# Retention scores as 64x64 matmuls in the four quarters of the TensorE array

## The chip, the core and the metric

The kernel runs on one core of one Trainium2 chip. The metric is the device time of one execution in microseconds; lower is better. Times are the median of several executions. A profiled execution is one more execution, with its own time and a trace of every instruction.

## What is computed

Three stages follow each other: a retention (attention with a decayed state) over 4 batches, 8 heads, 768 steps and 64 dimensions a head, and two feed-forward blocks over the 3072 tokens. Only the retention is touched by the change.

```python
gamma = 1.0 - 2.0 ** (-5.0 - np.arange(H, dtype=np.float32))
scale = 1.0 / np.sqrt(D)
for t in range(S):
    state = gamma[None, :, None, None] * state + np.einsum('bhd,bhe->bhde', k[:, :, t], v[:, :, t])
    y[:, :, t] = scale * np.einsum('bhd,bhde->bhe', q[:, :, t], state)
...
x = np.ascontiguousarray(attn_out.transpose(0, 2, 1, 3)).reshape(B * S, H * D)
x = _moe_ref(x=x, **moe_kwargs)
return _moe2_ref(x=x, **moe2_kwargs)
```

## The kernel before

The retention is done in 24 units: 4 batches of 6 chunks of 128 steps, all 8 heads of a chunk together. A unit's inputs are one tile `unit` of 1 MB: q and k transposed (the first half, one load of 512 KB), then k and v by tokens (the second half, another). SyncE's queue issues the loads (L478). Five such tiles exist (`UNITS`), and the load of unit u+4 is issued when unit u-1 has been used up, so four units' loads can be outstanding. The same 16 DMA engines also carry the weights of the first feed-forward block (`raw`, L123, from GpSimd's queue).

What TensorE does, in program order, is `scores(0)`, `scores(1)`, `outputs(0)`, `scores(2)`, `outputs(1)` and so on:

- `scores(u)` (L487): eight f32 matmuls, one for each head, k transposed (64 rows by 128 columns) against q transposed (64 by 128). Heads lie in pairs, one in rows 0 to 63 of the array (a = 0, results in one PSUM bank), the other in rows 64 to 127 (a = 1, the other bank). The result tile `sc` has one buffer. VectorE multiplies it by the causal mask into `pt` (L496), which also frees `sc`.
- `outputs(u)`: eight matmuls of `vs` with `pt` (L544, 128 rows by 64 columns), eight that add to the state `dp` (L555, 128 by 64; left out in the last chunk of a batch), and eight of the state `st` with q (L566, 64 by 64; left out in the first chunk of a batch). In L566 two successive heads pairs use all four quarters of the array: (rows 0-63, columns 0-63), (64-127, 64-127), (64-127, 0-63), (0-63, 64-127).

Each f32 matmul shows in the trace as two weight loads and two matmuls, so eight of them make 16 records of each. `vs` (v with its decay factors) is made by ScalarE in eight pieces of one head (L511), or by GpSimd (L506) in some units. `st` is a copy of `dp` by ScalarE (L560). VectorE scales the output `yp` (L579, L583, L586) and, from unit 12 on, spends most of the rest on converting the weights (L134, L139, L147, L167).

After the last unit the first feed-forward block starts on TensorE with L643, and from there on TensorE works through matmuls of 128x128 by 512 columns to the end.

Of the kernel before, what the change touches and what calls it, by code (L numbers as in the profile page):

```python
# [60 lines left out]
def tile_retention_then_two_ffns(  # L61
# [10 lines left out]
    nc = tc.nc  # L72
# [368 lines left out]
    with tc.manual_schedule():  # L441

        with (
# [36 lines left out]
            def scores(u):  # L480
                t = units[u]
                qk = t[:, 0:1024].rearrange("p (b n a i) -> p b n a i", b=2, n=2, a=2)
                v = t[:, 1536:2048].rearrange("p (h e) -> p h e", h=H)
                sc = aps.tile([P, 2, NP, P], F32, tag="sc", name=f"sc{u}", bufs=1)
                for p in range(NP):
                    for a in range(2):
                        nc.tensor.matmul(  # L487
                            sc[:, a, p, :],
                            qk[64 * a:64 * a + 64, p // 2, 1, p % 2, :],
                            qk[64 * a:64 * a + 64, p // 2, 0, p % 2, :],  # L490
                            start=True, stop=True,
                        )
                pt = att.tile([P, 2, NP, P], F32, tag="pt", name=f"pt{u}")

                def masked():
                    nc.vector.tensor_tensor(  # L496
                        out=pt.rearrange("p r a i -> p (r a) i"),
                        in0=sc.rearrange("p r a i -> p (r a) i"),
                        in1=mask_sb.unsqueeze(1).to_broadcast([P, H, P]),
                        op=ALU.mult,  # L500
                    )

                vs = att.tile([P, H, D], F32, tag="vs", name=f"vs{u}")
                if u < CPB or u % 3 == 0:

                    nc.gpsimd.tensor_tensor(  # L506
                        out=vs, in0=v, in1=vtab_sb[:, u % CPB, :].unsqueeze(2).to_broadcast([P, H, D]), op=ALU.mult
                    )
                else:
                    for h in range(H):  # L510
                        nc.scalar.mul(vs[:, h, :], v[:, h, :], vtab_sb[:, u % CPB, h:h + 1])  # L511
                pend[u] = (pt, vs)
                return masked
# [87 lines left out]
            for u in range(NU + 1):  # L601
                cv_high()
                masked = scores(u) if u < NU else None
                if u == 0:
                    fill = aps.tile([P, 2, NP, P], F32, tag="yp", name="fill")
                    for i in range(FILL):
                        nc.tensor.matmul(fill[:, 0, :, :], warm_sb[:, 0:P], warm_sb, start=True, stop=True)
                low = split_0()
                scaled = outputs(u - 1) if u > 0 else None
                if 0 < u < CPB:  # L610
                    for p in range(NP):
                        nc.scalar.mul(ytab_sb[u][:, p, :], ytab_sb[0][:, p, :], ystep_sb[:, u, p:p + 1])
                if masked is not None:
                    masked()
                if low is not None:
                    low()
                cv_unit(u)
                if scaled is not None:
                    scaled()
                cv_ahead(u)  # L620
                if u > 0:
                    load_unit(u + UNITS - 1)
# [141 lines left out]
        for n in range(NSTD):  # L764
            for f in range(NF):
# [8 lines left out]
                if n == 0 and f in (2, 3):  # L774
                    j = XHELD + f - 2
# [381 lines left out]
```

## Time and profile before

| what | value |
|---|---|
| three runs | 1040.97, 1044.02, 1045.16 us; median 1044.02 |
| the profiled execution | 1041.52 us, span of its trace 1039.8 us |
| granted TensorE clock | 1.0 of full speed throughout |
| busy, share of the span | TensorE matmul 99%, VectorE 73%, ScalarE 54%, GpSimd 12% |
| retention | from about 5 us to 82.7 us of the span |

An engine's busy time here is the union of its instructions' times. A busy TensorE is not one at its peak: a matmul's record runs from its start to the end of its pipeline, and the next may start long before that. How fast matmuls follow each other is therefore read from the starts: a merged row of 16 records that lasts 1.16 us, one record being 0.27 us, has 0.89 us from the first start to the last.

### The profile page before, as it was taken

Reading aid. Unit: us, or ns where it says so; the run is one execution under the profiler, and the core shown is the slowest. Engines: PE = TensorE matmul, PEld = TensorE weight load, DVE = VectorE, ACT = ScalarE, POOL = GpSimd, SP = SyncE. Lnnn points to the kernel's source line nnn. Section 1 sums busy time; section 2 is a strip of 40 time slices with the busy share of each in tenths; the row PEclk is TensorE's granted clock in tenths of the full one; section 3 lists DMA queues with packets and bytes.
Section 4 is the critical chain, followed back from the end, with each engine's and each line's share of the span. In section 5 each row is a group of like instructions: output and inputs, shape, how many; then the busy total and the mean of one; then the engine's idle time right before and its main releaser. Section 6 shows DMA issues by size and latency. Waiting matters only on the chain.

```text
span 1039.8 us, 15581 instructions
## 1 busy us (share of the span) xinstructions
PE 1028.8 (99%) x5602; PEld 849.1 (82%) x5602; DVE 762.5 (73%) x1059; ACT 559.1 (54%) x906; POOL 119.7 (12%) x183
## 2 busy tenths in 40 slices
PE   9999999999999999999999999999999999999998
PEld 6888888888888888888788888788888888888886
DVE  5798998798898888567787566887445986355953
ACT  4677775344766365556455688464233464234442
POOL 3121210111333000112000111000100001000000
PEclk9999999999999999999999999999999999999999
DMA  9995898865898867999867898767866667776664
GB/s 348 404 404 174 270 313 298 308 229 223 268 349 286 312 208 227 329 338 351 276 213 229 309 369 299 272 210 236 296 193 194 203 204 229 219 194 193 207 198 162
DMA packets 114637, 274.04 MB, mean 264 GB/s; under 512 B 12160, under 2 KB 12288, under 8 KB 114304
## 3 DMA queue, kind: packets, MB, share of 16 engines
q1 hardware_dynamic: 87008, 171.32, 50.0%
q0 software_dynamic: 26976, 100.67, 27.6%
q8 instruction: 45, 0.74, 0.3%
q10 hardware_dynamic: 576, 1.05, 0.3%
q14 instruction: 32, 0.26, 0.1%
HBM read 199.59 MB, written 73.40 MB: 263 GB/s over the span
## 4 chain that ended last, share of the span: by engine, by line
PE 82%; DMA 2%; DVE 0%; issue 0%
PE D L843 36%; PE X L843 16%; PE Z L843 8%; PE Y L843 4%; PE h L797 3%; PE h L795 3%; PE h L796 3%; DMA r<-kw 2%; PE y L676 2%; PE y L674 2%; PE y L675 2%; PE h L643 2%; PE h L645 1%; PE h L644 1%; DVE o L981 0%
## 5 line engine op out<-in xcount | busy, mean ns | idle before, releaser
L843 PE MATMUL D<-gx,r 128*128 128x512 f32 x1680 | 383.7, 390 | 2.9 <-DMA r<-kw 2.9
L843 PEld LDWEIGHTS D<-gx,r 128*128 128x128 f32 x1680 | 314.7, 188 | 70.8 <-DMA r<-kw 4.6
L947 DVE TENSOR_TENSOR gx<-g,gx 128x1024 fp32r<-128x1024 f32 x140 | 170.6, 1221 | 49.8 <-ACT gx L946 49.2
L946 ACT CAST gx<-g 128x1024 fp32r<-128x1024 f32 x140 | 145.1, 1050 | 110.2 <-PE D L843 97.4
L843 PE MATMUL X<-xh,r 128*128 128x512 f32 x512 | 157.7, 389 | 0.0
L864 ACT COPY g<-X 128x512 f32<-128x512 f32 x96 | 56.3, 586 | 154.6 <-PE X L843 154.4
L869 DVE TENSOR_TENSOR g<-Z,g 128x512 f32<-128x512 f32 x64 | 44.2, 691 | 123.0 <-ACT g L864 93.6
L843 PEld LDWEIGHTS X<-xh,r 128*128 128x128 f32 x512 | 96.0, 188 | 20.1 <-ACT g L864 0.2
L843 PE MATMUL X<-xl,r 128*128 128x512 f32 x256 | 99.6, 389 | 0.0
L843 PE MATMUL Z<-xh,r 128*128 128x512 f32 x256 | 78.8, 389 | 0.0
L843 PEld LDWEIGHTS Z<-xh,r 128*128 128x128 f32 x256 | 48.0, 188 | 10.0
L843 PEld LDWEIGHTS X<-xl,r 128*128 128x128 f32 x256 | 48.1, 188 | 10.0
L643 PE MATMUL h<-hl,w 128*128 128x512 f32 x128 | 50.2, 392 | 0.4 <-DVE w L167 0.4
L644 PE MATMUL h<-hl,w 128*128 128x512 f32 x128 | 49.9, 390 | 0.0
L645 PE MATMUL h<-hl,w 128*128 128x512 f32 x128 | 49.8, 389 | 0.0
L676 PE MATMUL y<-gl,w 128*128 128x512 f32 x128 | 49.8, 389 | 0.0
L674 PE MATMUL y<-gh,w 128*128 128x512 f32 x128 | 49.8, 389 | 0.0
L675 PE MATMUL y<-gh,w 128*128 128x512 f32 x128 | 49.8, 389 | 0.0
L795 PE MATMUL h<-hl,w 128*128 128x512 f32 x128 | 49.8, 389 | 0.0
L796 PE MATMUL h<-hl,w 128*128 128x512 f32 x128 | 49.8, 389 | 0.0
L797 PE MATMUL h<-hl,w 128*128 128x512 f32 x128 | 49.8, 389 | 0.0
L843 PE MATMUL Z<-xl,r 128*128 128x512 f32 x128 | 49.8, 389 | 0.0
(107 smaller groups left out, 1604.5 us busy)
## 6 DMA issues: line engine op xcount, KB each, us to landing
r<-kw SPq DMA_DIRECT2D x504, 256.0 KB, 3.0
kw<-wq POOLq DMA_DIRECT2D x32, 896.0 KB, 6.5
unit<-qkv SPq DMA_DIRECT2D x48, 512.0 KB, 9.0
raw<-w POOLq DMA_DIRECT2D x32, 512.0 KB, 6.3
kw<-wh POOLq DMA_DIRECT2D x16, 1024.0 KB, 4.7
kw<-w SPq DMA_DIRECT2D x16, 512.0 KB, 5.0
raw<-win POOLq DMA_DIRECT2D x16, 512.0 KB, 6.5
raw<-wout POOLq DMA_DIRECT2D x16, 512.0 KB, 7.2
```

The costliest lines, as they stand in the source:

```text
L643: nc.tensor.matmul(hp, lo[:, k], xh, start=(k == 0), stop=False)
L644: nc.tensor.matmul(hp, hi[:, k], xh, start=False, stop=False)
L645: nc.tensor.matmul(hp, hi[:, k], xl, start=False, stop=(k == KD - 1))
L674: nc.tensor.matmul(a, lo[:, e], gh, start=s0, stop=False)
L675: nc.tensor.matmul(a, hi[:, e], gh, start=False, stop=False)
L676: nc.tensor.matmul(a, hi[:, e], gl, start=False, stop=s1)
L795: nc.tensor.matmul(hp, lo[:, k], xh, start=(k == 0), stop=False)
L796: nc.tensor.matmul(hp, hi[:, k], xh, start=False, stop=False)
L797: nc.tensor.matmul(hp, hi[:, k], xl, start=False, stop=(k == KD - 1))
L843: nc.tensor.matmul(a, w, b, start=start, stop=stop, skip_group_check=True)
L946: nc.scalar.copy(out=hi, in_=src)
L947: v.tensor_tensor(out=lo, in0=src, in1=hi, op=ALU.subtract)
```

## The change

Each of the eight score matmuls of a unit (64 rows, 128 columns) becomes two of 64 rows by 64 columns. The first half gives output partitions 0 to 63, the second 64 to 127, from the same q. The order is: head pair, then row half a, then column half j. A unit's scores thus take 16 matmuls (32 records) in place of eight (16 records), and each pair of heads uses all four quarters of the array. What the matmuls write and where is the same, and no other line is changed; the changed file is one line longer.

```diff
                 for p in range(NP):
                     for a in range(2):
-                        nc.tensor.matmul(
-                            sc[:, a, p, :],
-                            qk[64 * a:64 * a + 64, p // 2, 1, p % 2, :],
-                            qk[64 * a:64 * a + 64, p // 2, 0, p % 2, :],
-                            start=True, stop=True,
-                        )
+                        for j in range(2):
+                            nc.tensor.matmul(
+                                sc[64 * j:64 * j + 64, a, p, :],
+                                qk[64 * a:64 * a + 64, p // 2, 1, p % 2, 64 * j:64 * j + 64],
+                                qk[64 * a:64 * a + 64, p // 2, 0, p % 2, :],
+                                start=True, stop=True, skip_group_check=True,
+                            )
```

On TensorE's queue a middle unit of the retention reads so before (a row is a line, the tile written and those read, the output's partitions by columns, how many in a row, and what is waited for):

```order
L566 MATMUL yp_307<-unit_160,st_267 64x128 x8
L487 MATMUL sc_348<-unit_167 128x128 [waits DMAHW2_49,DVE_49]
L487 MATMUL sc_348<-unit_167 128x128 x7
L544 MATMUL yp_364<-pt_300,vs_301 64x128 [waits Pool_49]
L544 MATMUL yp_364<-pt_300,vs_301 64x128 x7
```

and in the changed kernel:

```order
L567 MATMUL yp_339<-unit_160,st_291 64x128 x8
L488 MATMUL sc_380<-unit_167 64x128 [waits DMAHW2_49,DVE_49]
L488 MATMUL sc_380<-unit_167 64x128 x15
L545 MATMUL yp_404<-pt_332,vs_333 64x128 [waits Pool_49]
L545 MATMUL yp_404<-pt_332,vs_333 64x128 x7
```

Nothing moved: the scores stand between the same neighbours, and their first matmul still waits for a load of the unit (DMAHW) and for VectorE, which frees `sc`.

## Rows read from the trace of the kernel before

**Rows 1.** The page's busy time, share of the span and instructions of each engine.

```profile
PE 1028.8 (99%) x5602; PEld 849.1 (82%) x5602; DVE 762.5 (73%) x1059; ACT 559.1 (54%) x906; POOL 119.7 (12%) x183
```

**Rows 2.** Stretches of 4 us: each engine's busy time, clock, DMA share, GB/s.

```profile
28.00:32.00 4.00, 4.00 (x76) 3.69 (x74) 3.06 (x6) 3.08 (x13) 0.00 (x0) 1.00 1.02 403
...
68.00:72.00 4.00, 3.45 (x72) 3.05 (x72) 3.96 (x7) 4.00 (x14) 0.00 (x0) 1.00 1.03 407
76.00:80.00 4.00, 4.00 (x85) 3.64 (x82) 3.62 (x5) 3.83 (x16) 0.41 (x1) 1.00 1.00 390
80.00:84.00 4.00, 4.00 (x72) 3.20 (x69) 3.53 (x7) 2.67 (x7) 0.53 (x1) 1.00 0.32 111
```

**Rows 3.** TensorE's matmul groups, 0 to 83 us: busy us, mean ns | idle before.

```profile
L487 PE MATMUL sc<-unit 64*128 64x128 f32 x384 | 28.5, 286 | 2.1 <-DMA unit<-qkv 1.4 <-DVE w L167 0.5
L544 PE MATMUL yp<-pt,vs 128*64 128x128 f32 x384 | 26.3, 279 | 0.0
...
L566 PE MATMUL yp<-unit,st 64*64 64x128 f32 x320 | 13.3, 282 | 0.0
```

**Rows 4.** Timeline, units 21 to 23: start, length, engine, instructions [idle before].

```profile
71.51 1.16 PE L487 MATMUL sc<-unit 64*128 64x128 f32 x16 [0.55 <-DMA unit<-qkv]
...
74.09 0.67 PE L566 MATMUL yp<-unit,st 64*64 64x128 f32 x16
...
74.69 0.97 PEld L487 LDWEIGHTS sc<-unit 64*128 64x128 f32 x16 [0.17 <-DVE hm L139]
74.69 1.16 PE L487 MATMUL sc<-unit 64*128 64x128 f32 x16
...
75.78 1.09 PE L544 MATMUL yp<-pt,vs 128*64 128x128 f32 x16
...
75.90 1.23 DVE L496 TENSOR_TENSOR pt<-sc,tab_sb 128x1024 f32<-128x1024 f32 x1
...
76.71 0.64 PE L555 MATMUL dp<-vs,unit 128*64 128x64 f32 x16
...
77.27 0.67 PE L566 MATMUL yp<-unit,st 64*64 64x128 f32 x16
...
77.87 1.16 PE L487 MATMUL sc<-unit 64*128 64x128 f32 x16
...
78.63 2.02 ACT L511 ACTIVATE vs<-unit,tab_sb 128x64 f32<-128x64 f32 x8 [0.17 <-DMA unit<-qkv]
...
78.96 1.09 PE L544 MATMUL yp<-pt,vs 128*64 128x128 f32 x16
79.08 1.23 DVE L496 TENSOR_TENSOR pt<-sc,tab_sb 128x1024 f32<-128x1024 f32 x1 [0.38 <-PE sc L487]
...
81.05 1.09 PE L544 MATMUL yp<-pt,vs 128*64 128x128 f32 x16
...
82.67 0.50 PE L643 MATMUL h<-hl,w 128*128 128x512 f32 x1
```

**Rows 5.** Load of unit 22's q and k: issue, then time to landing.

```profile
L478 SPq DMA_DIRECT2D unit<-qkv x1: 328/328/328, 64.9 to 64.9; - x1
...
DMA to landing us min/median/max: 9.0/9.0/9.0
```

**Rows 6.** The same for unit 23's q and k.

```profile
L478 SPq DMA_DIRECT2D unit<-qkv x1: 328/328/328, 67.9 to 67.9; - x1
...
DMA to landing us min/median/max: 8.6/8.6/8.6
```

**Rows 7.** L566's matmuls alone, in steps of 0.11 us: busy (xrecords in flight).

```profile
64.15:64.30 0.15, 0.12 (x4) 1.00 1.02 410
64.30:64.41 0.11, 0.11 (x8) 1.00 0.84 335
64.41:64.52 0.11, 0.11 (x12) 1.00 1.22 489
```

**Rows 8.** Waits of TensorE after 83 us: total, times, longest.

```profile
PE h L643 <- DVE w L167: 0.4, 2, 0.2
```

## The prediction

> **What bounds the kernel now.** The first view is the page's table of engines: TensorE's matmuls fill 99% of the span [rows 1], so work on TensorE is worth something only where TensorE itself is what is waited for. The second is the retention, cut into stretches of 4 us. TensorE is busy nearly throughout, but so are the DMA engines: their share is 1.02 at 28 us, 1.03 at 68 us and 1.00 at 76 us, at about 400 GB/s, and falls to 0.32 only when the retention's loads are done [rows 2]. The stretches between that are not shown read alike. So two things are near their limit together, and the question is which ends last. The group of the score matmuls answers it: 2.1 us of idle TensorE before them, 1.4 of it ended by a landing of `unit` [rows 3]. The last such wait is that of unit 21, whose scores start at 71.51 us, 0.55 us after TensorE ran dry, released by the load [rows 4]. From there the chain is TensorE's alone: the units follow at 74.69 and 77.87 us, 3.18 us apart, with no idle matmul time in their rows, up to L643 at 82.67 us [rows 4].
>
> The reader should see in the timeline what the 3.18 us are made of. The scores take 1.16 us as a row; one record is about 0.27 us, so 0.89 us from the first start to the last. L566 just ahead of them (77.27 us, 0.67 us long) starts its last record at 77.67, and the scores start at 77.87: 0.20 us later. From L544 to L555 (75.78 + 1.09 - 0.27 = 76.60, then 76.71) it is 0.11 us. L544 and L555 have the same tile shape, 128x64; L566 and the scores do not, 64x64 and 64x128. The weight loads show the same gap of 0.17 us before the scores. It is put down to a VectorE instruction, but the mask that frees `sc` was long done, so I read it as the price of a change of shape.
>
> **The change part by part.** L566 has exactly the new shape, 64x64 with 128 columns streaming, in all four quarters. Its records come four at a time: 4, 8 and 12 in flight in successive steps, so four more each 0.11 us [rows 7]. The new scores are 32 records, eight such groups of four. Before, eight groups of two came in 0.89 us, also about 0.11 us apart. So the split buys no throughput of its own: two records of half the columns take the slot of one. What it saves is at the start:
>
> - Behind L566, the shape no longer changes. From L566's last start to the scores' last start was 0.20 + 0.89 = 1.09 us; with groups running on it is 8 x 0.11 = 0.88. Saved: 0.21 us.
> - From a standing start (behind a load, or where L566 is left out), L566's own 16 records take 0.67 - 0.27 = 0.40 us, so 32 take 0.40 + 4 x 0.11 = 0.84 against 0.89. Saved: 0.05 us, since the first weight loads are half as wide.
> - The change of shape from the scores to L544 stays.
>
> Of the 24 units 18 have L566 ahead of their scores (not the first two, nor the four behind a batch's first chunk). If everything reached the end it would be 18 x 0.21 + 6 x 0.05 = 4.1 us. That is the far end of the gain; the near end is nothing.
>
> I take a value near the small end, because of unit 21. Its scores start when their data land, and the DMA engines are full from 4 to 80 us with a fixed number of bytes. A TensorE that is ahead waits longer there. So what was saved before unit 21 is lost, and the sum starts anew at 71.51 us:
>
> - Unit 21, from a standing start: 0.05.
> - Unit 22, behind L566: 0.21 more, 0.26 in all. It would start at about 74.5 us; its data were issued at 64.9 and landed 9.0 us later, at 73.9 [rows 5], so they do not bind.
> - Unit 23, behind L566: 0.47 in all. It would start at about 77.5 us; its data are there at 67.9 + 8.6 = 76.5 [rows 6]. `sc` is free when the mask of unit 22 ends, 75.90 + 1.23 = 77.13 us; that mask followed other VectorE work without idle time [rows 4] and hardly moves, but it is early enough. Even with scores of no cost the data would allow only 77.87 - 76.6 = 1.3 us.
>
> What is late next: unit 23's `vs`, on ScalarE from 78.63 to 80.65 us, started by a landing [rows 4], so it does not move. L544 of unit 23 would start at 80.58 in place of 81.05 us. It takes `vs` head by head, a piece each quarter of a microsecond, and needs the last piece some 0.6 us after its start, so this stays hidden, with 0.5 us to spare. The mask of unit 23 (79.08 us, behind 0.38 us of waiting for the scores) moves with the scores. L643 then starts at 82.2 us. In the feed-forward part TensorE waits for converted weights twice, 0.4 us in all [rows 8]; these waits could take back some of it, but most of the conversion starts again behind TensorE's own results. I keep 0.5 us.
>
> **The sum**: 1041.52 - 0.5 = 1041.0 us against the profiled execution. That one lies 2.5 us below the median of the three runs; against the median it is 1044.02 - 0.5 = **1043.5 us**. The three runs span 4.2 us, 0.4% of the time, so a measurement tells nothing under about 0.5% (5.2 us) from no change.
>
> **The rivals.**
>
> *All of the saving arrives*: 1044.0 - 4.1 = 1039.9 us. The loads are issued when a tile comes free, so a faster TensorE issues them sooner. But issue is not what is short: a load lies 8.6 to 9.0 us in the queue [rows 5, 6] while the engines are full [rows 2]. Chance 4%.
>
> *None arrives*: the waits for converted weights, or landings a little later, take the 0.5 us back, 1044.0 us. The two waits of 0.4 us [rows 8] speak for it. Chance 25%.
>
> *The halves of one row block go one after the other*: in the new order the first two matmuls use the same rows and different columns, with the same q. If they take turns, the scores need 16 steps of 0.11 us in place of eight, 0.87 us a unit more, less the 0.05 to 0.21 saved: some 0.8 x 24 = 19 us, less the 2.1 us that TensorE idled before the scores anyway [rows 3]: 1061 us. It becomes slower by 0.5% once the scores cost 0.3 us a unit more ((5.2 + 2.1) / 24). Against it: in L566 too each row block carries two of the four records of a group, and the groups are 0.11 us apart [rows 7]; only the order within four differs, and q is not shared there. Chance 5%. [...]
>
> That the split is merged again or does nothing is excluded by the queue: 16 matmuls stand where eight stood.
>
> **How the numbers follow.** The forecast, 0.5 us less, has 66%; with the 25% of "none arrives" it lies within 0.5%. The full saving, 0.4%, also lies mostly within it; I give faster by over 0.5% 2%, slower 5%, and the rest 93%. The range goes from 1040.0 (the full saving, or about the lowest of the three runs less 0.5) to 1046.5, as far above the forecast as the lowest run lies below the median; the serial rival is left out.
>
> **What would show it.** In the changed kernel's timeline the scores should be 32 records, about 1.05 us long behind L566 and 1.1 from a standing start, with the scores' first start about 0.1 us behind L566's last and no gap of 0.17 us in the loads. The idle time ended by landings of `unit` should grow from 1.4 to some 3 to 5 us, unit 21 should still start close to 71.5 us, and L643 at about 82.2 us. The prediction is wrong if unit 21 starts over 1 us earlier (then loads came sooner), or if the scores' row lasts well over 1.2 us (then the quarters do not run together).

## The result: 0.95% slower, and the profile after

Six runs of the changed kernel had a median of 1053.62 us (1051.77 to 1055.62), six of the kernel before 1043.97 us. The ratio is 1.0095, 95% interval 1.0077 to 1.0112: slower, where no change that can be measured was forecast. The profiled execution took 1053.41 us.

The page's busy line and one of its instruction queues, q8 (packets, MB, share of 16 engines):

```profile
PE 1030.7 (98%) x5986; PEld 849.8 (81%) x5986; DVE 765.3 (73%) x1059; ACT 559.2 (53%) x906; POOL 120.1 (11%) x183
...
q8 instruction: 48, 0.79, 0.3%
```

Beside [rows 1] TensorE has 384 more matmuls and as many more weight loads (5986 against 5602). q8 carried 48 packets; the kernel before has 45 and 0.74 MB there. A packet is 16 KB (0.79 MB in 48 of them). So 768 more records go with three more packets, 256 records a packet; e5 below, with 384 more, has 46 packets, and e10, with 192 more, 45. The other instruction queue, q14, has 32 packets in both kernels. So q8 is read as TensorE's.

The score matmuls themselves came out as forecast. Their steps of 0.11 us, in the same form as [rows 7]:

```profile
62.00:62.11 0.11, 0.11 (x16) 1.00 0.38 149
62.11:62.22 0.11, 0.11 (x16) 1.00 0.74 298
```

The groups of four follow each other without a break, and a unit's 32 records take 1.05 us as a row. That is the figure that the forecast gave. The loss is elsewhere. TensorE's matmul groups of the retention (beside [rows 3]; L488, L545, L556, L567 and L644 are L487, L544, L555, L566 and L643 of the kernel before, one line further down):

```profile
L488 PE MATMUL sc<-unit 64*64 64x128 f32 x768 | 27.9, 276 | 4.5 <-issue 3.1 <-DMA unit<-qkv 1.3
L545 PE MATMUL yp<-pt,vs 128*64 128x128 f32 x384 | 27.8, 283 | 3.9 <-issue 3.9
L567 PE MATMUL yp<-unit,st 64*64 64x128 f32 x320 | 14.1, 283 | 2.1 <-issue 2.1
L556 PE MATMUL dp<-vs,unit 128*64 128x64 f32 x320 | 13.7, 226 | 1.2 <-issue 1.2
```

There are 10.3 us of idle time before matmuls of all four kinds put down to "issue", which means that the profile shows nothing that TensorE waited for. In [rows 3] L544 and L566 had none. The timeline shows where such a pause falls:

```profile
43.31 0.82 PE L545 MATMUL yp<-pt,vs 128*64 128x128 f32 x12
43.97 0.28 PE L556 MATMUL dp<-vs,unit 128*64 128x64 f32 x3
45.41 0.57 PE L556 MATMUL dp<-vs,unit 128*64 128x64 f32 x13 [1.16 <-issue]
45.91 0.67 PE L567 MATMUL yp<-unit,st 64*64 64x128 f32 x16
46.40 1.05 PE L488 MATMUL sc<-unit 64*64 64x128 f32 x32
...
48.89 1.05 PE L488 MATMUL sc<-unit 64*64 64x128 f32 x32
49.87 0.43 PE L545 MATMUL yp<-pt,vs 128*64 128x128 f32 x2
52.63 1.43 PE L545 MATMUL yp<-pt,vs 128*64 128x128 f32 x13 [2.32 <-issue]
```

The queue stops in the middle of a group, after 3 of 16 records of L556 and after 2 of 16 of L545. L545 takes `vs` head by head, so ScalarE could be what it waits for; but all of this `vs` was made by 51.10 us, 1.5 us before the restart at 52.63:

```profile
49.08 2.02 ACT L512 ACTIVATE vs<-unit,tab_sb 128x64 f32<-128x64 f32 x8 [1.47 <-DMA unit<-qkv]
```

Stretches cut inside successive pauses count the records between them (matmuls, then weight loads):

```profile
27.00:33.00 6.00, 5.23 (x127) 4.41 (x127) 4.50 (x7) 3.90 (x16) 0.00 (x0) 1.00 1.01 399
33.00:38.70 5.70, 5.00 (x126) 4.45 (x126) 2.59 (x5) 1.61 (x7) 2.11 (x3) 1.00 0.98 351
38.70:45.00 6.30, 5.18 (x126) 4.64 (x127) 3.68 (x6) 3.74 (x16) 0.00 (x0) 1.00 0.99 339
45.00:51.50 6.50, 4.90 (x127) 4.07 (x127) 4.56 (x8) 3.56 (x11) 1.58 (x2) 1.00 0.97 371
```

Each has 252 to 254 records; with the two to four separate waits that TensorE's queue holds in 1.6 units (one ahead of the scores, one ahead of L556) this fits 256 instructions each time. Counted one by one in the trace, with the separate waits, TensorE's queue has 705 instructions before the first of the nine restarts put down to issue, and 961, 1217, 1473, 1729, 1985, 2753, 3009 and 3265 before the others: the steps are 256, and once three times 256. A 16 KB packet of q8 divided by 256 is 64 bytes an instruction, as an estimate. So in this trace TensorE stopped where a packet's worth of instructions ends. Ahead of the restart at 33.58 us such a packet moved; the DMA queues between 31.2 and 32.3 us:

```profile
q1 hardware_dynamic: 80, 0.31, 70.7%
q0 software_dynamic: 43, 0.13, 28.8%
q8 instruction: 1, 0.02, 5.0%
```

It is the same at all nine restarts: a packet of q8 ended 1.2 to 1.6 us earlier. So TensorE stood at these places until its packet had come, and went on at about the same distance behind it each time. The packets also tell why the pace changed. At those nine places the packet began to move 3.0 to 4.8 us after the previous count of 256 was passed, and moved for about 1 us, so that 256 instructions took 5.5 to 7.2 us. In the kernel before, at the same counts between 18 and 80 us, the packets began 2.7 to 4.6 us after the previous one, hardly sooner. But TensorE took 6.1 to 7.7 us over 256 instructions there, and the packet had landed 1.4 to 3.0 us before it was needed. The kernel before had little room left.

L644 then starts at 92.09 us, where L643 started at 82.67 [rows 4]: 9.4 of the 11.9 us between the two profiled executions.

### The profile page after: what moved, and what is told of

It is laid out like the page before. It is cut to its first block, busy times and chain, and to the rows that moved or that the text cites. A ratio compares the mean times of both kernels' runs of the same rounds, so it can differ in the third digit from the quotient of the medians.

```text
span 1051.5 us, 16349 instructions
## 1 busy us (share of the span) xinstructions
PE 1030.7 (98%) x5986; PEld 849.8 (81%) x5986; DVE 765.3 (73%) x1059; ACT 559.2 (53%) x906; POOL 120.1 (11%) x183
## 3 DMA queue, kind: packets, MB, share of 16 engines
q10 hardware_dynamic: 576, 1.05, 0.3%
## 4 chain that ended last, share of the span: by engine, by line
PE 81%; DMA 2%; DVE 0%; issue 0%
PE D L844 36%; PE X L844 16%; PE Z L844 8%; PE Y L844 4%; PE h L798 3%; PE h L797 3%; PE h L796 3%; DMA r<-kw 2%; PE y L677 2%; PE y L676 2%; PE y L675 2%; PE h L644 1%; PE h L646 1%; PE h L645 1%; DVE o L982 0%
## 5 line engine op out<-in xcount | busy, mean ns | idle before, releaser
L644 PE MATMUL h<-hl,w 128*128 128x512 f32 x128 | 50.2, 392 | 0.4 <-DVE w L167 0.2
L645 PE MATMUL h<-hl,w 128*128 128x512 f32 x128 | 49.9, 390 | 0.0
```

Of the source, the lines that this page charges most:

```text
L644: nc.tensor.matmul(hp, lo[:, k], xh, start=(k == 0), stop=False)
L645: nc.tensor.matmul(hp, hi[:, k], xh, start=False, stop=False)
```

## The experiments

Two theories stood against each other. Theory A: TensorE runs out of instructions, since each further f32 matmul is four records more to fetch, through DMA engines that are full of unit loads. Theory B: the split costs time on TensorE itself. "L643" in the table is the first matmul of the feed-forward part (its line differs from kernel to kernel); "issue" is the sum of the idle time before matmuls put down to issue in the retention. Two columns hold what the theories differ in: score records a unit, and the mean DMA share from 5 to 80 us. Each ratio is to executions of the kernel before that were made beside the run; their median was 1042.62 us for e1 to e4, 1042.59 for e5 to e8 and 1042.93 for e9 and e10. It is an estimate over all executions and not just the quotient of two medians.

| kernel | score records a unit | DMA share | issue, us | L643, us | median, us | ratio to before (95%) |
|---|---|---|---|---|---|---|
| before | 32 | 1.02 | 0 | 82.67 | 1043.97 | |
| split (after) | 64 | 0.99 | 10.3 | 92.09 | 1053.62 | 1.0095 (1.0077 to 1.0112) |
| e1_split_half | 64 | 0.76 | 2.6 | 83.25 | 1042.43 | 1.0003 (0.9985 to 1.0021) |
| e2_base_half | 32 | 0.77 | 0 | 81.41 | 1040.26 | 0.9976 (0.9961 to 0.9992) |
| e3_split_bf16 | 32 | 1.01 | 3.3 | 82.94 | 1042.34 | 0.9996 (0.9981 to 1.0012) |
| e4_base_bf16x4 | 64 | 1.00 | 7.8 | 91.34 | 1050.53 | 1.0082 (1.0054 to 1.0110) |
| e5_split_odd | 48 on average | 0.99 | 5.3 | 89.43 | 1050.28 | 1.0080 (1.0052 to 1.0107) |
| e6_split_noload | 64 | 0.40 | 0 | 80.64 | 1039.80 | 0.9964 (0.9951 to 0.9978) |
| e7_base_noload | 32 | 0.40 | 0 | 82.75 | 1040.79 | 0.9992 (0.9982 to 1.0002) |
| e8_split_units3 | 64 | (0.77 to 119 us) | 0 | 119.80 | 1080.30 | 1.0367 (1.0342 to 1.0393) |
| e9_split_units4 | 64 | 0.97 | 9.4 | 94.93 | 1054.36 | 1.0099 (1.0074 to 1.0124) |
| e10_split_quarter | 40 on average | 1.02 | 1.9 | 84.37 | 1042.82 | 0.9992 (0.9977 to 1.0007) |

**Half of the loads (e1, e2).** The same edit in both kernels:

```diff
-units[u] = att.tile([P, 2048], F32, tag="unit", name=f"unit{u}", bufs=UNITS)
+units[u] = att.tile([P, 1024], F32, tag="unit", name=f"unit{u}", bufs=UNITS)
+if u < UNITS:
+    kv[u] = att.tile([P, 1024], F32, tag=f"kv{u}", name=f"kv{u}", bufs=1)
...
-nc.sync.dma_start(out=units[u][:, a:z], in_=qkv[u, :, a:z])
+if a < 1024:
+    nc.sync.dma_start(out=units[u][:, a:z], in_=qkv[u, :, a:z])
+elif u < UNITS:
+    nc.sync.dma_start(out=kv[u][:, a - 1024:z - 1024], in_=qkv[u, :, a:z])
...
```

(`scores` and `outputs` then read v and k by tokens from `kv[u % UNITS]`.)

> The split kernel with half of the unit loads: the second half of a unit (k and v by tokens) is loaded only for the first five units and used again for the later ones, so 1 MB a unit becomes 0.5 MB and the outputs are those of other data. Theory A (TensorE runs out of instructions: 160 records a unit, fetched in pieces of 256 records through DMA engines that are full of loads, some 6 us a piece): with the engines no longer full a piece comes sooner, the pauses at every 256th record go, and the kernel is as fast as or faster than the unsplit one with the same half loads, 1034 to 1039 us. Theory B (the split matmuls themselves, or their change of shape, cost TensorE some 0.4 us a unit, whatever the DMA does): about 10 us slower than the unsplit one with half loads, 1046 to 1050 us.

> The unsplit kernel with the same half loads, the control of the run before. Both theories: TensorE's own pace of 3.18 us a unit without the waits for landings, some 3 to 6 us less than the kernel before, 1038 to 1041 us.

The difference of about 10 us shrank to 2.2 us between the medians. So the loads decide most of it, against theory B. But theory A had expected no difference at all, and e1's 1042.43 us lies between its range and that of theory B. The trace has 2.6 us of issue pauses left, with the DMA share still at 0.76; whether these are all of the 2.2 us is what e6 and e7 ask.

**Records against shape (e3, e4).** The scores read the upper halves of the f32 words as bf16, which makes a matmul two records in place of four (e3's scores show 384 matmul records, the split kernel's 768). e3 applies it to the split kernel, e4 to the old shape with each matmul issued four times:

```diff
+qb = t[:, 0:1024].bitcast(BF16).rearrange("p (b n a i w) -> p b n a i w", b=2, n=2, a=2, w=2)
-for p in range(NP):
+for p in [p for p in range(NP) for _ in range(4)]:
...
-        qk[64 * a:64 * a + 64, p // 2, 1, p % 2, :],
-        qk[64 * a:64 * a + 64, p // 2, 0, p % 2, :],
+        qb[64 * a:64 * a + 64, p // 2, 1, p % 2, :, 1],
+        qb[64 * a:64 * a + 64, p // 2, 0, p % 2, :, 1],
```

> The split kernel with the scores from the upper halves of the f32 words taken as bf16 (less exact scores): the same 16 matmuls of 64x64 in the same order and quarters, but each is 2 records in place of 4, so the scores are 32 records of loads and matmuls a unit as in the kernel before, in place of 64. Theory A: the fetch keeps up as in the kernel before, 1041 to 1045 us. Theory B in the form that the quarters or their order are the cost: slower than before still, 1047 us or more.

> The old shape, 64x128, with the scores from the upper halves of the words as bf16, and every matmul issued four times over (the last one stands): 64 records a unit as in the split kernel, with array work about that of the kernel before and no quarter of the array used in a new way. Theory A: pauses at every 256th record as in the split kernel, 1049 to 1058 us. Theory B: as the kernel before, 1041 to 1046 us.

This tells the theories apart. The quarters with the old number of records are no slower (0.9996). The old shape with the new number of records is slower by nearly as much as the split (1.0082, 7.9 us between the medians). The pauses of e4 fall like those of the split kernel, in the middle of a group, and its stretches between pauses hold 127 matmuls and 127 loads:

```profile
34.50:40.50 6.00, 5.05 (x127) 4.34 (x127) 2.74 (x5) 1.77 (x7) 2.12 (x3) 1.00 1.00 363
40.50:47.50 7.00, 5.23 (x127) 4.69 (x127) 3.21 (x4) 3.19 (x13) 0.00 (x0) 1.00 1.03 364
```

One of the pauses in e4's timeline, after nine of the 16 records of L556:

```profile
45.96 0.45 PE L556 MATMUL dp<-vs,unit 128*64 128x64 f32 x9
48.12 0.45 PE L556 MATMUL dp<-vs,unit 128*64 128x64 f32 x7 [1.71 <-issue]
```

e4's q8 has 48 packets, as many as the split kernel, and e3's has 45, as many as the kernel before.

e3 shows one thing more. Its scores need less array time (11.0 us busy, 27.9 in the split kernel), and TensorE spent what it saved in waiting for landings (the waits, us in total, times, longest):

```profile
PE sc L489 <- DMA unit<-qkv: 10.2, 9, 2.7
PE sc L489 <- issue: 2.1, 2, 1.2
PE sc L489 <- DVE pt L498: 0.9, 2, 0.5
```

It reached the feed-forward part at 82.94 us all the same. Because of this slack e3 alone could hide a cost of the quarters; that there is none is shown by the scores' row of 1.05 us and by e6 below. And its 3.3 us of issue, with the old number of records, fall at the same counts of 256, each 1.3 to 1.5 us after a packet of q8: it is the pace at which TensorE uses records up that counts, and their number matters through it.

**No loads (e6, e7).** From the sixth unit on, the first five tiles are used again:

```diff
-units[u] = att.tile([P, 2048], F32, tag="unit", name=f"unit{u}", bufs=UNITS)
+units[u] = units[u - UNITS] if u >= UNITS else att.tile([P, 2048], F32, tag=f"unit{u}", name=f"unit{u}", bufs=1)
-for a, z in zip(parts, parts[1:]):
+for a, z in (zip(parts, parts[1:]) if u < UNITS else ()):
...
-t = units.pop(u)
+t = units[u]
```

> The split kernel with the unit loads taken away from the sixth unit on: the first five tiles are used again and again (outputs of other data), so that in the retention only the weights of the next stage are loaded. Theory A: hardly any pause at the 256th records is left, and the 0.05 to 0.21 us a unit that the forecast gave for the shape come out where VectorE does not bind: 1 to 4 us less than the unsplit kernel without loads, 1035 to 1039 us. If the 2 us by which the split kernel was slower with half loads are a cost of the split itself: 2 us more than the unsplit one, 1041 us or more.

> The unsplit kernel with the same loads taken away, the control of the run before. TensorE's own pace, as with half loads: 1038 to 1041 us by both.

With the DMA share at 0.40 no issue pause is left in either kernel, and the split one is ahead: the feed-forward part starts at 80.64 us against 82.75, and the median is 1.0 us lower (the intervals of the two ratios do not overlap). e6's 1039.80 us lies between the two ranges of its expectation, nearer to the first. The packets explain it: in e6 they began to move at most 2.3 us after the previous count of 256, nine times of 13 within 0.6 us, and landed 1.6 to 5.3 us before they were needed. The only waits of 12 to 95 us before e6's matmuls:

```profile
PE sc L488 <- DVE pt L497: 1.9, 4, 0.9
```

So the rest of 2.2 us in e1 was no price of the split. What the split saves on TensorE is real, 2.1 us in this pair of traces, of the 4.1 us that the forecast's sum gave for all units; a part of the rest went into these waits for VectorE.

**How many units (e5, e10).** The split in every second unit, and in every fourth:

```diff
-for j in range(2):
+n = 64 if u % 2 else 128
+for j in range(P // n):
```

(`u % 4 == 1` in e10, and `n` in place of 64 in the slices.)

> Only every second unit (the odd ones) has the split scores; all outputs as before. On average 144 records a unit. Theory A: a fetch of 256 records takes some 6.2 us while the DMA engines are full; some 3,240 records to the end of the retention are 12.6 pieces, 78 us, which is just about the retention's own length of 78 us, so most of the loss is gone: 1042 to 1046 us. Theory C (a cost of each split unit, 9.6 / 24 = 0.4 us, whatever its neighbours are): half the loss, 1046.5 to 1049 us.

> The split scores in six units only (1, 5, 9, ...), 192 records more than before, all outputs as before. With twelve such units the kernel was 7.7 us slower, with 24 it was 9.6, so the loss is neither a threshold nor a price per unit. Theory A2 (before the change the fetch just keeps up with TensorE, so that each further 256 records cost a whole fetch of 6 to 7 us until the pauses thin out the loads): 192 records, 0.75 of a fetch, 1046 to 1048 us. Theory A as first put, with room left before the change: 1042 to 1044 us.

Both of my numbers for a fetch fell. From e5's expectation, theory A with a fixed 6.2 us a fetch gave 1042 to 1046; it measured 1050.28, above the 1046.5 to 1049 of a price per unit too, though its four executions (1048.11 to 1053.94 us) don't exclude that one. I then took the kernel before to be just at the edge (theory A2), and e10 contradicted that: six split units cost nothing that can be measured. What does grow in step is the issue time, 0, 1.9, 5.3 and 10.3 us for 0, 192, 384 and 768 more records. In e10 it is small beside the waits that the kernel before has anyway; that it is hidden there for this reason is argued, not shown (its trace reaches L645 at 84.37 us, 1.7 us later than the kernel before). Theory A2 was right in part: in the kernel before, a packet landed 1.4 to 3.0 us before its use, where 1.2 to 1.6 went by at each restart of the changed kernel, so the room, as an estimate, was between nothing and some 1.6 us a packet. I have no rule that gives the time of a fetch beforehand.

**Fewer loads outstanding (e8, e9).** The split kernel with `UNITS = 3` and `UNITS = 4`:

> The split kernel with three unit tiles in place of five, so that at most two units' loads are outstanding in place of four. Theory A with the fetch waiting behind all that is queued: pieces come sooner, fewer pauses, 1044 to 1050 us. Theory A with the fetch getting its turn among the queues, however long they are: pauses as in the split kernel, 1051 to 1056 us, or more if the loads come late.

> The split kernel with four unit tiles in place of five: three units' loads outstanding in place of four, at a pace of some 3.6 us a unit time enough for a landing of 8 to 9 us. If a fetch waits behind what is queued, pieces come sooner: pauses at the 256th records well under the 12.6 us of the split kernel, 1045 to 1051 us. If it only gets its share of full engines: pauses as before, 1051 to 1056 us. If the loads come late as with three tiles, waits for landings in place of the pauses, 1055 us or more.

e8 missed its question: with three tiles the loads come late, and it measures that alone. The wait of e8's trace from 12 to 120 us:

```profile
PE sc L488 <- DMA unit<-qkv: 31.1, 14, 4.3
```

With four tiles the pauses stay (9.4 us of issue), and waits for landings come on top (3.6 us in the group of the scores). A shorter line of loads did not bring the instructions sooner: the packets began 2.0 to 5.8 us after the previous count of 256. What holds their start back while the engines are full stays open.

No run points to a version that is faster than the kernel before: e3 and e10 are level with it, and e2 and e6 leave loads out.

## Why the prediction was wrong

- **The step that failed** is the costing of the split itself: "So the split buys no throughput of its own: two records of half the columns take the slot of one. What it saves is at the start". The 32 further records a unit were priced by array time alone. That they are also fetched (48 packets of q8 in place of 45), by the same DMA engines that the forecast had just read as full [rows 2], had no term. The term was zero; it measured 10.3 us of issue time in the changed kernel, and in e4, with the array's work in the old shape, 7.8 us of issue time and 7.9 us of the whole time. So in the forecast's sum the gain could shrink to nothing, but only a cost on the array (the rival of 1061 us) could make the kernel slower.
- **The slower rival had the wrong mechanism.** It let the halves of one row block take turns, 1061 us. The trace after shows four records each 0.11 us, though the halves share their row block, and e6, which reaches the feed-forward part 2.1 us ahead of e7, shows that the new order costs nothing on TensorE. The direction of that rival, slower, came true, but for another reason.
- **The sizes on the array were right**: 1.05 us for 32 records, and behind L567 the scores' first start (46.40 us) came 0.09 us after L567's last (45.91 + 0.67 - 0.27 = 46.31), where it had been 0.20. The saving comes out where instructions do not lack (e6 against e7).
- **"So what was saved before unit 21 is lost"**, to landings, held in e3, where TensorE had time to spare and waited for landings. In the changed kernel it never came to that: TensorE was the late one, it waited 1.3 us for landings in place of 1.4, not the 3 to 5 us foretold, unit 21's scores started at 79.39, not close to 71.5 us, and L644 at 92.09, not 82.2 us. The two signs that the prediction named for being wrong, unit 21 over 1 us earlier or a row of scores well over 1.2 us, did not show (at full clock and without a pause inside, a row took 1.05 us): it failed in a way that it had not thought of.
- **The rest of the loss**, 2.5 us of the 11.9 between the profiled executions, arose after L644, and goes with the clock, not with the split. From L644 to the end of the trace it is 959.4 us, and 957.1 from L643 before. In the changed kernel's trace the granted clock fell in that part, behind waits for `r` of 1.13 and 1.00 us, to 0.66 of full speed on average over 4 us (0.50 from 668 to 670 us); before, it was 1.0 throughout. In all runs the traces with such a stretch of lower clock between 500 and 672 us (the split kernel, e3, e5, e6) have 958.7 to 960.9 us there, and those without (the kernel before, e1, e2, e4, e7 to e10) 956.0 to 957.1. e1, e8, e9 and e10 have split scores too; whether the split makes such stretches more frequent is not shown. The kernel before differs in the same way from one execution to the next: 1040.43 us at a mean granted clock of 1.0, 1046.71 at 0.997.
- **The clock within the retention** also fell once, to 0.61 on average in the stretch that follows the longest pause, of 2.32 us; the scores at 55.06 us took 1.69 us there in place of 1.05, and this is part of the 9.4 us. The stretches (the clock is the third number from the end):

```profile
52.00:56.00 4.00, 3.37 (x50) 3.25 (x53) 1.44 (x3) 0.84 (x2) 0.00 (x0) 0.61 1.00 372
...
660.00:664.00 4.00, 4.00 (x19) 3.11 (x17) 2.47 (x3) 1.56 (x3) 0.00 (x0) 1.00 1.02 405
664.00:668.00 4.00, 1.87 (x6) 1.13 (x6) 2.19 (x3) 3.34 (x6) 0.00 (x0) 0.91 1.04 400
668.00:672.00 4.00, 4.00 (x14) 3.15 (x13) 3.13 (x3) 1.02 (x1) 0.00 (x0) 0.66 0.43 152
```

From 668 us 14 matmuls are in flight in 4 us, where 19 were from 660.

## What to carry to other kernels

In these runs a matmul cost its instructions as well as its array time (10.3 us of issue time at a DMA share of 0.99, none at 0.40): count the records that a stage issues, and where the DMA engines are near a share of 1, ask whether the next 256 of them arrive in time. An f32 matmul counted four here (768 more records for 192 more matmuls), so splitting the f32 matmuls of the scores in two doubled the records for the same work, 64 a unit in place of 32. Idle time put down to "issue", in the middle of a group and at equal counts of records, was the sign; halving the data loads, or making more records in the old shape, told it from a cost of the engine.

## What the runs showed of the hardware that was not expected

- In these traces TensorE's instructions come in packets of 16 KB, 256 at a time, and a packet that came late stopped the engine at the boundary, for up to 2.3 us of idle matmul time. At all nine such pauses of the changed kernel the packet had ended 1.2 to 1.6 us before the restart.
- In the split kernel the issue time grew with the share of the DMA engines: none at 0.40 (e6), 2.6 us at 0.76 (e1), 10.3 us at 0.99 (the changed kernel). At 0.77 in e8, which waited 31.1 us for landings, there was none.
- With q8 at 0.3% of the engines' time over the whole span, the cost in these runs is not the bandwidth that instructions take. Nor is it the packet's own transfer: 0.9 to 1.4 us in the changed kernel's retention, 0.9 to 1.3 with a DMA share of 0.40 (e6). What differs is how late it begins to move: at the pauses 3.0 to 4.8 us after TensorE passed the previous count of 256, in e6 at most 2.3.
